# Attention, MLP and routed experts on one core: the products with v in one piece, behind the last copy, and routing logits as one accumulation

## Chip, cores and metric

The kernel runs on one core of one Trainium2 chip. The metric is device time in microseconds (us) of one execution, as a median of several runs. One execution was also recorded by the hardware profiler; every duration below comes from that one.

## What is computed

Three layers follow each other. Cut to what matters here:

```
# 1. attention, 4 batches x 8 heads, 576 tokens, head size 64, only the 32 largest scores of a row
scores = (q @ k.T) / 8
kth    = 32nd largest of each row
attn   = softmax(where(scores >= kth, scores, -1e9))
x      = attn @ v                                # then heads side by side: [2304, 512]

# 2. MLP
h = x @ w_in;  y = (h * clip(h + 3, 0, 6) / 6) @ w_out      # 512 -> 2048 -> 512

# 3. one expert of 8 for each token
logits = normalize(y) @ normalize(expert_emb).T / tau
e      = argmax(logits);  gate = softmax(logits)[e]
out    = gate * (relu(y @ w1[e]) @ w2[e])        # 512 -> 1024 -> 512
```

## The kernel before

**Units.** Attention is cut into 72 units: 64 take 128 query rows of a pair of heads, 8 take the 64 rows that are left over (rows 512 to 575) of two pairs of heads. A main loop (`while i < NU + 3 or moe or side`) starts one unit in each turn and keeps three in flight, one for each of the three score tiles `s` (`sbuf[i % 3]`).

**The path of one unit.** `scores` (L310) multiplies q with k on TensorE, in two halves `g` of 288 keys, into the PSUM tile `ps_sc`, of which there is one; ScalarE copies each half to `s` (L311). VectorE folds the halves (L317 to L321, reading `ps_sc`) and finds the 32 largest (`select`, L335, L341). `mask` pushes the others down (ScalarE L360, GpSimd L361) and takes the exponential (ScalarE L364). `transposes` scales the rows by the reciprocal of their sum (GpSimd L376), turns the nine blocks of 128 keys (two heads of 576 keys make 1152) on TensorE into `bank_t`, three at a time (L381), and ScalarE copies each three to `pt` (L382). `values` multiplies `pt` with v (L394) into a half of the PSUM bank `bank_a`; `finish` copies the sum to `x` (L412).

**The products with v.** A unit of 128 rows has ten, five for each head. Head `n` writes PSUM partitions 64n to 64n+63, so its weights are 64 columns wide, and the two heads use two halves of the array. Of the nine blocks of `pt`, head 0 reads 0 to 4 and head 1 reads 5 to 8 and 4. Blocks 0 to 2 come with the first copy, 3 to 5 with the second, 6 to 8 with the third. The loop begins with `k = 0`: block 0 (first copy), then block 5 (second copy), then 1, then 6 (third copy). A left-over unit has twenty products, on 64 moving columns each.

**The filler.** When 128 rows of x are complete, `push_group` puts nine steps of the MLP on a queue: `s1` (L433, into the two banks `bank_h`) and `s2` (L452, into `y`). Two steps go with each unit. After the last step come the routing steps r1 to r5 of that group, on a queue of their own. r1 transposes y to `yt` (L477, L479). r2 (L486) multiplies the normalized embeddings with `yt` in four products, each of 32 weight columns into its own 32 PSUM partitions; ScalarE copies the 128 rows to `lt` (L488). r3 (L492) adds the four parts by a product with the constant `fold`, which also brings tokens to the partitions, and VectorE copies the logits to `l_all` (L493). r4 and r5 find each token's place in its expert's list. There are 18 groups.

**What sets the order.** A list scheduler plays the program at build time and puts the instructions of each engine in a fixed order, which the engine follows in that order. What is ready goes by priority; `tc.high_priority(offset=...)` raises it. The offsets stand at the top: `FINISH = 500`, `MASK = 100`, `TURN = 300`, `VALUES = 300`, `SCORES = 500`, `SELECT = 600`, and `AHEAD = 600` for the steps between `s1` and `s2`.

**After attention.** The experts follow, the largest first: gathers of token rows (L631, L635), `stage1` (L734), `stage2` (L747), scattered rows of the output (L754).

Of the kernel before, what the change touches and what calls it, by code (L numbers as in the profile page):

```python
# [9 lines left out]
F32 = mybir.dt.float32  # L10
# [5 lines left out]
ALU = mybir.AluOpType  # L16
# [6 lines left out]
E, F2 = 8, 1024  # L23
# [20 lines left out]
PREP2 = 400  # L44
MASK = 100
TURN = 300
VALUES = 300
FINISH = 500
SCORES = 500
SELECT = 600  # L50
# [20 lines left out]
def layers(ctx: ExitStack, tc: tile.TileContext, qt, kt, v, w_in, w_out, embt, tau, w1, w2, out, y_dram, g_dram, x_dram, tbl, flag):  # L71
    nc = tc.nc
    exact = flag is None

    const = ctx.enter_context(tc.tile_pool(name="const", bufs=1))
    ident = const.tile([128, 128], F32, name="ident")
# [3 lines left out]
    ones = const.tile([128, 128], BF16, name="ones")  # L80
    tri = const.tile([128, 128], BF16, name="tri")
    ids = const.tile([128, NG, 2], I32, name="ids")
    ent = const.tile([128, 4, 32], F32, name="ent")
    fold = const.tile([128, E], F32, name="fold")
    acc = const.tile([128, E], BF16, name="acc")
    l_all = const.tile([128, NG, E], F32, name="l_all")
    ss_all = const.tile([128, NG], F32, name="ss_all")
# [3 lines left out]
    m1 = ctx.enter_context(tc.tile_pool(name="m1", bufs=1))  # L91
# [14 lines left out]
    bank_h = [ps_h.tile([128, 512], F32, name=f"bank_h{i}") for i in range(2)]  # L106
# [4 lines left out]
    def half_a():  # L111
        turn[0] ^= 1
        return bank_a[:, turn[0], :]
# [11 lines left out]
    def embed():  # L125
        onesf = xp.tile([128, 128], F32, tag="x", name="onesf")
        nc.vector.memset(onesf, 1.0)

        et = fs.tile([128, 4, E], F32, tag="df", name="et")
        nc.sync.dma_start(out=et, in_=embt.rearrange("(k p) e -> p k e", p=128))  # L130
        tb = fs.tile([128, 1], F32, tag="gt", name="tb")
        nc.sync.dma_start(out=tb, in_=tau.rearrange("(o t) -> o t", o=1).broadcast_to([128, 1]))
        sq = fs.tile([128, 4, E], F32, tag="gts", name="sq")
        nc.vector.tensor_tensor(sq, et, et, op=ALU.mult)
        pe = half_a()
        for k in range(4):
            nc.tensor.matmul(pe[:, :E], onesf, sq[:, k, :], start=(k == 0), stop=(k == 3))
        nr = fs.tile([128, E], F32, tag="nrm", name="nr")
        nc.scalar.activation(nr, pe[:, :E], AF.Sqrt)
        nc.vector.tensor_scalar(nr, nr, 1e-6, tb[:, 0:1], op0=ALU.add, op1=ALU.mult)  # L140
        nc.vector.reciprocal(nr, nr)
        nc.vector.memset(ent, 0.0)
        nc.vector.tensor_tensor(ent[:, :, 0:E], et, nr.unsqueeze(1).broadcast_to([128, 4, E]), op=ALU.mult)

    def setup():
        make_identity(nc, ident)
        nc.vector.tensor_tensor(fold, ident[:, 0:E], ident[:, 32:32 + E], op=ALU.add)
        for k in (2, 3):
            nc.vector.tensor_tensor(fold, fold, ident[:, 32 * k:32 * k + E], op=ALU.add)
        nc.vector.memset(half, 0.5)  # L150
        nc.vector.memset(ones, 1.0)
        nc.vector.memset(acc, 0.0)
        nc.gpsimd.iota(iota8, pattern=[[1, 8]], base=0, channel_multiplier=0, allow_small_or_imprecise_dtypes=True)
        nc.gpsimd.iota(ebase, pattern=[[STRIDE, 8]], base=0, channel_multiplier=0, allow_small_or_imprecise_dtypes=True)
        nc.gpsimd.affine_select(tri, ones, pattern=[[1, 128]], compare_op=ALU.is_gt, fill=0.0, base=0, channel_multiplier=-1)
        nc.gpsimd.iota(ids[:, :, 0], pattern=[[128, NG]], base=0, channel_multiplier=1)
        nc.gpsimd.iota(ids[:, 0:16, 1].rearrange("p (b t) -> p b t", b=4), pattern=[[S, 4], [128, 4]], base=0, channel_multiplier=1)
        for hf in range(2):
            nc.gpsimd.iota(ids[64 * hf:64 * hf + 64, 16:18, 1], pattern=[[2 * S, 2]], base=hf * S + 512, channel_multiplier=1)
        padt = xp.tile([128, E * STRIDE * 2 // 128], I32, tag="x", name="padt")  # L160
        nc.gpsimd.memset(padt, PAD)
        nc.sync.dma_start(out=tbl.rearrange("(p a) b -> p (a b)", p=128), in_=padt)
        zr = xp.tile([128, DM], F32, tag="x", name="zr")
        nc.vector.memset(zr, 0.0)
        nc.sync.dma_start(out=y_dram[NT:NT + 1, :], in_=zr[0:1, :])
        for g in (14, 15):
            nc.sync.dma_start(out=y_dram[128 * g:128 * g + 128, :], in_=zr)
        nc.sync.dma_start(out=g_dram[NT:NT + 128, :].rearrange("p o -> o p"), in_=zr[0:1, 0:128])
        embed()
# [196 lines left out]
    def transposes(i):  # L366


        e = sbuf[i % 3].rearrange("p n s -> p (n s)")
        pts[i] = ptp.tile([128, 9, 128], F32, tag="pt", name="pt")  # L370
        rv = sums.pop(i)
        nc.gpsimd.tensor_scalar(rv, rv, 1e-9, None, op0=ALU.add)
        nc.vector.reciprocal(rv, rv)  # L373
        for n in range(2):
            x = tile_of(i, n)
            nc.gpsimd.tensor_scalar(x, x, rv[:, n:n + 1], 1.0, op0=ALU.mult, op1=ALU.mult)  # L376
        for c in range(0, 9, 3):
            turn[1] ^= 1
            pp = bank_t[turn[1]]
            for k in range(3):  # L380
                nc.tensor.transpose(pp[:, 128 * k:128 * k + 128], e[:, 128 * (c + k):128 * (c + k) + 128], ident)  # L381
            nc.scalar.copy(pts[i][:, c:c + 3, :].rearrange("p k n -> p (k n)"), pp[:, :384])  # L382

    def values(i):


        u = units[i]
        pt = pts.pop(i)
        av = half_a()[:, :128]
        vs = [(V[u[1], u[3]], 0, 128)] if u[0] == "t" else [(V[u[1], u[2] + a], 64 * a, 64 * a + 64) for a in range(2)]  # L390
        for vt, c0, c1 in vs:
            for k in range(5):
                for n in range(2):
                    nc.tensor.matmul(av[64 * n:64 * n + 64, c0:c1], vt[:, k, 64 * n:64 * n + 64],  # L394
                                     pt[:, k + 5 * n if k < 4 else 4, c0:c1], start=(k == 0), stop=(k == 4))

        def finish():
            if u[0] == "r":
                _, b, p0 = u
                xq = mp.tile([128, 2, 64], F32, tag="xq", name="xq", bufs=1)  # L400
                nc.scalar.copy(xq.rearrange("d a t -> d (a t)"), av)
                nc.sync.dma_start(out=x_dram[p0:p0 + 2, :, 64 * b:64 * b + 64].rearrange("n d t -> d n t"), in_=xq)
                if b == B - 1 and p0 == 2:
                    for g in range(2):
                        X = xp.tile([128, 4, 128], F32, tag="x", name="x")
                        nc.sync.dma_start(out=X, in_=x_dram[:, :, 128 * g:128 * g + 128].rearrange("k d t -> d k t"))
                        push_group(X, 16 + g)
                return
            _, b, t, p = u
            if p == 0:  # L410
                xt[b, t] = xp.tile([128, 4, 128], F32, tag="x", name="x")
            nc.scalar.copy(xt[b, t][:, p, :], av)  # L412
            if p == 3:
                push_group(xt.pop((b, t)), 4 * b + t)
        return finish
# [8 lines left out]
    def push_group(X, g):  # L424

        state = {}
# [53 lines left out]
            state["yt"] = yt  # L480

        def r2():

            pl = bank_h[1][:, 256:384]
            for k in range(4):
                nc.tensor.matmul(pl[32 * k:32 * k + 32, :], ent[:, k, :], state["yt"][:, k, :], start=True, stop=True)  # L486
            state["lt"] = m1.tile([128, 128], F32, tag="yt", name="lt")
            nc.scalar.copy(state["lt"], pl)  # L488

        def r3():  # L490
            p2 = bank_h[0][:, 384:392]
            nc.tensor.matmul(p2, state["lt"], fold, start=True, stop=True)  # L492
            nc.vector.tensor_copy(l_all[:, g, :], p2)  # L493
            ix = sm.tile([128, 8], U32, tag="ix", name="ix")
            ixf = sm.tile([128, 1], F32, tag="ixf", name="ixf")
            oh = sm.tile([128, E], BF16, tag="oh", name="oh")
            mx = sm.tile([128, 8], F32, tag="mx", name="mx")
            nc.vector.max(mx, l_all[:, g, :])
            nc.vector.max_index(ix, mx, l_all[:, g, :])
            nc.vector.tensor_copy(ixf, ix[:, 0:1])  # L500
            nc.vector.tensor_scalar(oh, iota8, ixf, None, op0=ALU.is_equal)
            state["oh"] = oh
# [153 lines left out]
    if True:  # L656
# [5 lines left out]
        with tc.high_priority(offset=0):  # L662
            setup()
# [4 lines left out]
        while i < NU + 3 or moe or side:  # L668
# [9 lines left out]
            if 0 <= i - 2 < NU:  # L678
                with tc.high_priority(offset=MASK):
                    mask(i - 2)  # L680
                with tc.high_priority(offset=TURN):
                    transposes(i - 2)
                with tc.high_priority(offset=VALUES):
                    fin = [f for f in [values(i - 2)] if f]
# [220 lines left out]
```

## Time and profile before

| | |
|---|---|
| median of 3 runs | 1204.87 us (1203.87 to 1205.3) |
| the profiled execution | 1204.7 us, of which its span is 1202.8 us |
| busy in the span | PE 1080.5 us (90%), weight loads 918.6 (76%), DVE 808.6 (67%), ACT 737.1 (61%), POOL 696.9 (58%) |
| mean granted TensorE clock | 0.971 of 2.4 GHz |
| products with v (L394) | 1600 matmul records, 50.1 to 841.8 us |
| routing products (L486, L492) | 144 and 36 matmul records |

PE is TensorE's matmuls, PEld its weight loads, DVE is VectorE, ACT is ScalarE, POOL is GpSimd, SP is SyncE. A product of two float32 operands (L433, L394, L486, L492) shows as two matmul records, one of float32r operands (L310, L452) or a transpose (L381) as one. A record's duration runs past the start of the next record, since matmuls are pipelined; what one costs in a row of its kind is the distance from start to start.

### The profile page before, as it was taken

What the parts mean: (1) busy time and instruction counts of PE and PEld (TensorE: products, weight loads), DVE (VectorE), ACT (ScalarE), POOL (GpSimd) and SP (SyncE); (2) the same over time, 40 slices, a digit from 0 to 9 for tenths busy, and PEclk for the clock granted to TensorE, in tenths of its full rate; (3) what the DMA queues carried; (4) which work ended last, traced back from release to release, by engine and by line L of the source; (5) the groups of instructions that cost most, each with busy time, mean ns of one, the idle gap of its engine ahead of it and who ended that gap; (6) DMA issues with size and microseconds to landing.
All of it is one profiled execution on the core that took longest, in us unless ns stands there. A gap on an engine that the chain in (4) does not pass through costs nothing. (4 is left out here: it accounts for less than half of the span.)

```text
span 1202.8 us, 22847 instructions
## 1 busy us (share of the span) xinstructions
PE 1080.5 (90%) x7836; PEld 918.6 (76%) x7836; DVE 808.6 (67%) x2690; ACT 737.1 (61%) x1646; POOL 696.9 (58%) x982
## 2 busy tenths in 40 slices
PE   2347799999999999999999999999999799999993
PEld 2235578778888788888887888888888688888882
DVE  7999987788778858877788877874133344444440
ACT  5655676876767777776787776766344244444440
POOL 7977985967666786666797756754231442212200
PEclk9967999999999999999999999999999899999996
DMA  8443310230000221101022001000040564344530
GB/s 270 141 136 114 124 33 6 71 91 23 28 10 26 58 74 45 32 6 30 28 69 59 15 23 34 21 10 10 10 167 10 182 197 146 127 168 152 175 139 21
DMA packets 71783, 92.75 MB, mean 77 GB/s; under 512 B 18319, under 2 KB 44066, under 8 KB 71647
## 3 DMA queue, kind: packets, MB, share of 16 engines
q1 hardware_dynamic: 67007, 81.00, 21.4%
q0 software_dynamic: 4640, 10.10, 2.5%
q8 instruction: 66, 1.08, 0.4%
q14 instruction: 70, 0.57, 0.2%
HBM read 80.37 MB, written 11.32 MB: 76 GB/s over the span
## 5 line engine op out<-in xcount | busy, mean ns | idle before, releaser
L433 PE MATMUL bank_h<-x,win 128*128 128x128 f32 x2304 | 311.6, 279 | 16.5 <-ACT x L412 7.4
L433 PEld LDWEIGHTS bank_h<-x,win 128*128 128x128 f32 x2304 | 291.0, 193 | 38.4 <-ACT x L412 9.2
L361 POOL TENSOR_TENSOR s<-s,z 128x576 f32<-128x576 f32 x144 | 184.2, 1295 | 42.3 <-ACT z L360 40.0
L335 DVE MAX8 A<-left 128x8 f32<-128x288 f32 (+1 forms) x288 | 162.2, 596 | 0.0
L442 POOL TENSOR_TENSOR gl<-u,gh 128x256 fp32r<-128x256 f32 x144 | 106.7, 745 | 82.2 <-ACT gh L441 79.9
L394 PE MATMUL bank_a<-pt,vt 128*64 128x128 f32 (+1 forms) x1600 | 142.0, 279 | 13.5 <-ACT pt L382 13.4
L394 PEld LDWEIGHTS bank_a<-pt,vt 128*64 128x64 f32 x1600 | 93.5, 139 | 53.5 <-ACT pt L382 17.7
L310 PE MATMUL ps_sc<-kst,qh 128*128 128x288 f32 x256 | 86.5, 351 | 47.2 <-DVE left L321 13.2
L452 PE MATMUL y<-wh,gh 128*128 128x512 f32 x288 | 123.1, 427 | 0.8 <-ACT gh L441 0.8
L382 ACT COPY pt<-bank_t 128x384 f32<-128x384 f32 x216 | 100.4, 480 | 35.9 <-PE bank_t L381 34.9
L452 PE MATMUL y<-wh,gl 128*128 128x512 f32 x288 | 121.1, 421 | 0.1
L360 ACT ACTIVATE z<-s,zb 128x576 bf16<-128x576 f32 x144 | 107.4, 775 | 21.5 <-DVE zb L350 18.7
L381 PE MATMUL bank_t<-ident,s 128*128 128x128 f32 x648 | 110.8, 289 | 7.8 <-POOL s L376 7.7
L364 ACT ACTIVATE s<-s,nb 128x576 f32<-128x576 f32 x144 | 112.5, 782 | 8.1 <-POOL s L361 7.9
L311 ACT COPY s<-ps_sc 128x576 f32<-128x576 f32 x144 | 91.7, 637 | 38.9 <-PE ps_sc L310 32.3
L376 POOL TENSOR_SCALAR s<-s,sums 128x576 f32<-128x576 f32 x144 | 108.9, 767 | 10.9 <-DVE sums L373 9.7
L452 PE MATMUL y<-wl,gh 128*128 128x512 f32 x288 | 114.2, 396 | 0.0
L616 DVE TENSOR_TENSOR l<-a,h 128x1024 fp32r<-128x1024 f32 x64 | 76.9, 1223 | 52.7 <-ACT h L615 52.3
L317 DVE TENSOR_TENSOR ps_sc<-ps_sc,s 128x288 f32<-128x288 f32 x72 | 33.3, 462 | 105.0 <-ACT s L311 104.9
L438 ACT ACTIVATE u<-bank_h,half 128x256 f32<-128x256 f32 x144 | 67.9, 475 | 58.1 <-PE bank_h L433 55.7
L439 DVE SCALAR_TENSOR_TENSOR u<-u,bank_h 128x256 f32<-128x256 f32 x144 | 59.3, 413 | 60.6 <-ACT u L438 59.8
L381 PEld LDWEIGHTS bank_t<-ident,s 128*128 128x128 f32 x648 | 75.3, 144 | 29.6 <-issue 14.9
(227 smaller groups left out, 2457.1 us busy)
## 6 DMA issues: line engine op xcount, KB each, us to landing
a<-in_moe_w_dram SPq DMA_DIRECT2D x64, 512.0 KB, 8.5
kraw<-in_k_dram SPq DMA_DIRECT2D x64, 144.0 KB, 2.4
qraw<-in_q_dram SPq DMA_DIRECT2D x64, 128.0 KB, 2.2
w<-in_moe_w_in_dram SPq DMA_DIRECT2D x32, 256.0 KB, 3.2
w<-in_moe_w_out_dram SPq DMA_DIRECT2D x32, 256.0 KB, 2.9
vt<-in_v_dram SPq DMA_DIRECT2D x16, 320.0 KB, 2.9
y_dram<-ysb SPq DMA_DIRECT2D x18, 256.0 KB, 2.1
qraw<-in_q_dram SPq DMA_DIRECT2D x16, 64.0 KB, 2.3
```

Of the source, the lines that this page charges most:

```text
L311: nc.scalar.copy(s[:, :, HS * g:HS * g + HS], ps[:, :, :HS])
L335: nc.vector.max(A[:, n, 8 * r:8 * r + 8], src[:, n, :w])
L360: nc.scalar.activation(zb_[n], s, AF.Relu, bias=zb[:, n:n + 1], scale=-BIG)
L361: nc.gpsimd.tensor_tensor(s, s, zb_[n], op=ALU.subtract)
L364: nc.scalar.activation(s, s, AF.Exp, bias=nb[:, n:n + 1], scale=SCALE, accum_out=so[:, n:n + 1])
L376: nc.gpsimd.tensor_scalar(x, x, rv[:, n:n + 1], 1.0, op0=ALU.mult, op1=ALU.mult)
L381: nc.tensor.transpose(pp[:, 128 * k:128 * k + 128], e[:, 128 * (c + k):128 * (c + k) + 128], ident)
L382: nc.scalar.copy(pts[i][:, c:c + 3, :].rearrange("p k n -> p (k n)"), pp[:, :384])
L394: nc.tensor.matmul(av[64 * n:64 * n + 64, c0:c1], vt[:, k, 64 * n:64 * n + 64], pt[:, k + 5 * n if k < 4 else 4, c0:c1], start=(k == 0), s ...
L433: nc.tensor.matmul(ph[:, a, :], win[:, k, 128 * f:128 * f + 128], X[:, k, :], start=(k == 0), stop=(k == 3))
L442: nc.gpsimd.tensor_tensor(gl, u, gh.bitcast(F32), op=ALU.subtract)
L452: nc.tensor.matmul(state["y"], x[:, a, :], w[:, f, :], start=(f == 0 and n == 0), stop=(f == 15 and n == 2))
```

## The change

`VALUES` goes from 300 to 1200, above every other offset. The loop over the five blocks of a head takes them as 3, 2, 1, 0, 4 with head 1 first, so that the first product reads block 8, which comes with the third copy.

r2 now has `yt` as weights, 128 columns wide, and the embeddings `ent` as the moving operand, 8 columns, in one accumulation of four products into `p2`, which lies in `bank_h[1]` where `pl` lay. ScalarE's copy `lt`, the product with `fold` and the making of `fold` are gone, and r3 begins with VectorE's copy to `l_all`. Lines behind the change move up by 4 to 8: L394 becomes L390, L310 L305, L381 L376, L433 L429, L452 L448, L486 L481.

```diff
-VALUES = 300
+VALUES = 1200
...
-    ent = const.tile([128, 4, 32], F32, name="ent")
-    fold = const.tile([128, E], F32, name="fold")
+    ent = const.tile([128, 4, E], F32, name="ent")
...
-        nc.vector.memset(ent, 0.0)
-        nc.vector.tensor_tensor(ent[:, :, 0:E], et, nr.unsqueeze(1).broadcast_to([128, 4, E]), op=ALU.mult)
+        nc.vector.tensor_tensor(ent, et, nr.unsqueeze(1).broadcast_to([128, 4, E]), op=ALU.mult)
...
-        nc.vector.tensor_tensor(fold, ident[:, 0:E], ident[:, 32:32 + E], op=ALU.add)
-        for k in (2, 3):
-            nc.vector.tensor_tensor(fold, fold, ident[:, 32 * k:32 * k + E], op=ALU.add)
...
-            for k in range(5):
-                for n in range(2):
+
+            for o, k in enumerate((3, 2, 1, 0, 4)):
+                for n in (1, 0):
                     nc.tensor.matmul(av[64 * n:64 * n + 64, c0:c1], vt[:, k, 64 * n:64 * n + 64],
-                                     pt[:, k + 5 * n if k < 4 else 4, c0:c1], start=(k == 0), stop=(k == 4))
+                                     pt[:, k + 5 * n if k < 4 else 4, c0:c1], start=(o == 0), stop=(o == 4))
...
         def r2():
-
-            pl = bank_h[1][:, 256:384]
+            p2 = bank_h[1][:, 256:264]
             for k in range(4):
-                nc.tensor.matmul(pl[32 * k:32 * k + 32, :], ent[:, k, :], state["yt"][:, k, :], start=True, stop=True)
-            state["lt"] = m1.tile([128, 128], F32, tag="yt", name="lt")
-            nc.scalar.copy(state["lt"], pl)
+                nc.tensor.matmul(p2, state["yt"][:, k, :], ent[:, k, :], start=(k == 0), stop=(k == 3))
+            state["p2"] = p2
 
         def r3():
-            p2 = bank_h[0][:, 384:392]
-            nc.tensor.matmul(p2, state["lt"], fold, start=True, stop=True)
-            nc.vector.tensor_copy(l_all[:, g, :], p2)
+            nc.vector.tensor_copy(l_all[:, g, :], state["p2"])
```

How this moves instructions stands in the built order of TensorE. In the order of before the 800 products with v stand in 205 pieces, with other products between them: 61 of one product, 51 of two, 46 of seven, and 47 of other sizes. In the order of the change they stand in 72 pieces, one for each unit.

TensorE, the products with v of the 40th unit. The names `s_...` are the score tile that is transposed, `bank_t_...` the two banks that take it. Before:

```order
L433 MATMUL bank_h_118<-x,win 128x128
L394 MATMUL bank_a<-pt,vt 64x128
L381 MATMUL bank_t_121<-ident,s_144 128x128 x3
L394 MATMUL bank_a<-pt,vt 64x128 x2
L310 MATMUL ps_sc<-kst,qh 128x288
...
L433 MATMUL bank_h_119<-x,win 128x128 x3
L394 MATMUL bank_a<-pt,vt 64x128 x7
L452 MATMUL y<-wh,gh 128x512
```

The same unit with the change:

```order
L376 MATMUL bank_t_120<-ident,s_143 128x128 x3
L429 MATMUL bank_h_118<-x,win 128x128 x3
L305 MATMUL ps_sc<-kst,qh 128x288
...
L390 MATMUL bank_a<-pt,vt 64x128 x10
L448 MATMUL y<-wh,gh 128x512
```

One product, two and seven became ten in a row, behind the last transposes, three MLP products and four of scores.

TensorE, the 31st unit, whose products with v, with the change, follow its last three transposes with nothing between them; a routing step r2 stands behind them. Before:

```order
L394 MATMUL bank_a<-pt,vt 64x128
L381 MATMUL bank_t_122<-ident,s_144 128x128 x3
L452 MATMUL y<-wh,gh 128x512
L452 MATMUL y<-wl,gh 128x512
L394 MATMUL bank_a<-pt,vt 64x128 x2
L452 MATMUL y<-wh,gl 128x512
```

With the change:

```order
L473 MATMUL bank_h_117<-ident,ysb 128x128 x4
L376 MATMUL bank_t_121<-ident,s_143 128x128 x3
L390 MATMUL bank_a<-pt,vt 64x128 x10
L481 MATMUL bank_h_118<-ent,yt 128x8 x4
L429 MATMUL bank_h_117<-x,win 128x128 x3
```

The ten products moved next to the transposes whose copy they read. Counted over the order of the change, four units stand so (the 18th, 22nd, 31st and 54th); from the seventh unit on, six more have four instructions in between, ten have five to eight, and the other 46 have more.

TensorE, a routing step r2 and r3 in the middle of attention. Before:

```order
L381 MATMUL bank_t_122<-ident,s_144 128x128 x2
L486 MATMUL bank_h_119<-yt,ent 32x128 x4
L433 MATMUL bank_h_118<-x,win 128x128 x3
...
L492 MATMUL bank_h_118<-fold,lt 128x8
L433 MATMUL bank_h_119<-x,win 128x128 x3
```

With the change:

```order
L305 MATMUL ps_sc<-kst,ql 128x288
L481 MATMUL bank_h_118<-ent,yt 128x8 x4
L429 MATMUL bank_h_117<-x,win 128x128 x8
```

The second product is gone, and the four products of r2 are 128 weight columns wide and 8 long.

## Rows read from the trace of the kernel before

**Rows 1.** Busy time by stretch: the stretch in us, its length, busy us (and records) of PE, PEld, DVE, ACT and POOL, the granted clock, the DMA share, GB/s.

```profile
0.00:150.00 150.00, 76.74 (x425) 59.15 (x426) 141.59 (x402) 88.32 (x213) 127.09 (x179) 0.86 0.50 157
500.00:700.00 200.00, 197.34 (x1572) 167.59 (x1572) 157.38 (x612) 148.58 (x349) 139.60 (x207) 1.00 0.13 36
900.00:1203.00 303.00, 270.01 (x1591) 235.62 (x1590) 121.35 (x203) 119.05 (x193) 71.13 (x74) 0.95 0.38 131
```

**Rows 2.** What TensorE waited for from 150 to 890 us: who waited, for whom, us in total, times, longest.

```profile
PE bank_h L433 <- ACT lt L488: 2.4, 2, 1.3
PE bank_a L394 <- ACT pt L382: 2.1, 4, 0.7
PE bank_t L381 <- POOL s L376: 1.2, 1, 1.2
```

**Rows 3.** What VectorE waited for from 200 to 800 us.

```profile
DVE ps_sc L317 <- ACT s L311: 96.0, 44, 5.1
```

**Rows 4.** The timeline of TensorE's matmuls: start and length in us, line, operation, out and in, weights and moving operand, number of records in a row. The 40th unit's products with v, in three pieces.

```profile
500.51 0.38 PE L433 MATMUL bank_h<-x,win 128*128 128x128 f32 x2
500.82 0.43 PE L394 MATMUL bank_a<-pt,vt 128*64 128x128 f32 x2
501.18 0.55 PE L381 MATMUL bank_t<-ident,s 128*128 128x128 f32 x3
501.66 0.44 PE L394 MATMUL bank_a<-pt,vt 128*64 128x128 f32 x4
502.03 0.40 PE L310 MATMUL ps_sc<-kst,qh 128*128 128x288 f32 x1
...
502.66 0.83 PE L433 MATMUL bank_h<-x,win 128*128 128x128 f32 x6
503.42 1.09 PE L394 MATMUL bank_a<-pt,vt 128*64 128x128 f32 x14
504.43 0.50 PE L452 MATMUL y<-wh,gh 128*128 128x512 f32 x1
504.77 0.40 PE L452 MATMUL y<-wl,gh 128*128 128x512 f32 x1
```

**Rows 5.** The same view where a unit's ten products, 20 records, stand in one piece.

```profile
720.48 0.40 PE L452 MATMUL y<-wl,gh 128*128 128x512 f32 x1
720.71 0.40 PE L452 MATMUL y<-wh,gl 128*128 128x512 f32 x1
721.04 1.31 PE L394 MATMUL bank_a<-pt,vt 128*64 128x128 f32 x20
722.28 0.94 PE L433 MATMUL bank_h<-x,win 128*128 128x128 f32 x6
722.98 1.31 PE L310 MATMUL ps_sc<-kst,zq 128*128 128x288 f32 x8
```

**Rows 6.** The same view, two stretches of full-width products alone.

```profile
327.95 0.61 PE L433 MATMUL bank_h<-x,win 128*128 128x128 f32 x4
328.40 0.82 PE L381 MATMUL bank_t<-ident,s 128*128 128x128 f32 x6
329.05 0.39 PE L433 MATMUL bank_h<-x,win 128*128 128x128 f32 x2
...
505.01 0.30 PE L310 MATMUL ps_sc<-kst,qh 128*128 128x288 f32 x1
505.14 0.29 PE L310 MATMUL ps_sc<-kst,ql 128*128 128x288 f32 x1
```

**Rows 7.** PE and PEld of the products with v (L394) from 0 to 150 us: busy us and records of each, granted clock, DMA share, GB/s.

```profile
0.00:150.00 150.00, 16.65 (x126) 10.42 (x126) 0.86 0.50 157
```

**Rows 8.** The timeline of TensorE's matmuls around one r2 (L486).

```profile
601.04 0.29 PE L310 MATMUL ps_sc<-kst,ql 128*128 128x288 f32 x1
601.26 0.43 PE L486 MATMUL bank_h<-yt,ent 128*32 128x128 f32 x8
601.62 2.05 PE L433 MATMUL bank_h<-x,win 128*128 128x128 f32 x16
603.50 0.82 PE L381 MATMUL bank_t<-ident,s 128*128 128x128 f32 x6
```

**Rows 9.** The same around one product of r3 (L492).

```profile
799.12 0.61 PE L433 MATMUL bank_h<-x,win 128*128 128x128 f32 x4
799.56 0.29 PE L492 MATMUL bank_h<-fold,lt 128*128 128x8 f32 x2
799.70 0.47 PE L433 MATMUL bank_h<-x,win 128*128 128x128 f32 x2
800.01 0.60 PE L381 MATMUL bank_t<-ident,s 128*128 128x128 f32 x4
```

**Rows 10.** The timeline of TensorE and ScalarE: the third copy of the 40th unit (its transposes start at 501.18), and the third transposes and copy of the unit behind it.

```profile
501.77 0.48 ACT L382 COPY pt<-bank_t 128x384 f32<-128x384 f32 x1 [1.40 <-PE bank_t L381]
509.81 0.55 PE L381 MATMUL bank_t<-ident,s 128*128 128x128 f32 x3
511.60 0.47 ACT L382 COPY pt<-bank_t 128x384 f32<-128x384 f32 x1
```

**Rows 11.** What TensorE waited for from 0 to 150 us.

```profile
PE bank_a L394 <- ACT pt L382: 11.3, 5, 3.1
PE bank_t L381 <- POOL s L376: 6.5, 3, 3.9
```

## Prediction

> **What bounds the kernel now.** I first read busy time by stretch. From 500 to 700 us TensorE is busy 197.34 of 200 us at a granted clock of 1.00, while VectorE is busy 157.38, ScalarE 148.58 and GpSimd 139.60; from 0 to 150 us it is the other way round, VectorE 141.59 and TensorE 76.74 [rows 1]. So the start belongs to VectorE and its suppliers, and from about 150 us to the end of the MLP near 890 us TensorE's own queue sets the pace. The experts, from 900 us, hold nothing that the change touches; they move forward or back as a whole. The list of waits confirms the middle: TensorE waited there for the copies of `pt` 2.1 us in all, for `lt` 2.4, for GpSimd's scaling 1.2 [rows 2]. VectorE in turn waited 96.0 us between 200 and 800 us for ScalarE's copy of the scores, which waits for TensorE [rows 3]. An instruction that TensorE can do without is therefore worth its whole time in the middle, until something else is late.
>
> Busy time does not show what is dear on TensorE, since it is near 100% in any case. I therefore read its timeline from start to start.
>
> **Prices of full-width products.** Four records of L433 take 328.40 - 327.95 = 0.45 us, 0.1125 each; six transposes 329.05 - 328.40 = 0.65, 0.108 each; one record of scores 505.14 - 505.01 = 0.13 [rows 6]; one of L452 720.71 - 720.48 = 0.23 [rows 5].
>
> **The products with v: what a piece costs.** The 40th unit's 20 records stand in pieces of 2, 4 and 14. From 500.51 to 504.77 us TensorE also did 8 records of L433 (0.90), 3 transposes (0.325), 4 of scores (0.52) and one of L452 (0.23). The rest, 4.26 - 1.975 = 2.285 us, is the products with v [rows 4]. Where 20 records stand in one piece, 720.71 to 722.98 us holds one L452 (0.23) and 6 of L433 (0.675) beside them; the rest is 2.27 - 0.905 = 1.365 us [rows 5]. Same work, 0.92 us less, for two pieces less: 0.46 us for each entry to and exit from the half-width products, together with the product that then runs without its partner in the other half. Entry and exit can be seen alone: from the last L452 to the first L394 are 0.33 us where 0.23 are usual [rows 5], and between the two L452 behind the piece of 14 lie 0.34 [rows 4].
>
> The order of the change has 72 pieces instead of 205, so 133 x 0.46 = 61 us of TensorE's time go. 126 of the 1600 records lie before 150 us [rows 7], where TensorE was idle half the time; that 8% is worth nothing. **56 us** remain on the path.
>
> **The products with v: the new wait.** All ten now stand behind the third copy. In the 40th unit the third transposes start at 501.18 [rows 4] and their copy ends at 501.77 + 0.48 = 502.25 us, 1.07 us later; the next unit's start at 509.81 and their copy ends at 511.60 + 0.47 = 512.07, 2.26 us later, since ScalarE was busy [rows 10]. The three transposes themselves are 0.33 of that, so a unit with nothing in between lets TensorE wait 0.74 to 1.93 us, and with it the scores and MLP products queued behind, on which ScalarE's copies and VectorE's selection depend. By the order of the change four units have nothing between (3.0 to 7.7 us), six have four instructions of at least 0.43 us together (6 x 0.2 to 6 x 1.5, or 1.2 to 9), ten have five to eight, near 0.9 us (0 to 10), the other 46 more. Ends: 4 and 27 us. I take **6**, near the low end, since TensorE waited for this copy only 2.1 us in four waits in this stretch [rows 2]. Of this wait little existed before, when two products or three could start with the earlier copies, so I count it in full.
>
> **What is late next.** If TensorE needs 8% less time, VectorE's 157.38 of 200 us become 157.38 of about 184, 85%; its wait for scores, 96.0 us in 600, is what pays [rows 1, 3]. It is no bound yet, but leads shrink, and some units' scaled scores will come after TensorE is ready for the transposes. Such a wait is 6.5 / 3 = 2.2 us where it happened at the start [rows 11], and happened once in the middle, for 1.2 us [rows 2]. One unit in twelve of the 66 behind the start gives 5.5 x 2.2 = **12 us**. The ends are 0 (TensorE keeps its order's slack) and one unit in four, 36 us. I choose low, because one wait moves all of TensorE's later work and so restores the lead of the units in flight.
>
> **The routing logits.** r2's eight narrow records cost, from 601.04 to 603.50 us, 2.46 less one of scores (0.13) and 16 of L433 (1.80): 0.53 us [rows 8]. r3's product: 799.12 to 800.01 us holds 6 records of L433, 0.675 of 0.89, so 0.215 us for its two records, 0.11 each [rows 9]. That record is 128 weight columns wide and 8 long, as the eight new ones of r2 are; they cost 8 x 0.11 = 0.86 us. Per group 0.86 - 0.53 - 0.215 = +0.12 us, in 18 groups **+2 us**. The wait for `lt`, 2.4 us, goes [rows 2]; VectorE's copy now holds the bank `bank_h[1]` in its place until it has read, so I count the waits as **0**, between -2.4 and +3. ScalarE is spared 18 copies and VectorE a few instructions at the start, both beside TensorE's work.
>
> A rule speaks against this edit. The rows show that four 32-column products save no time once entry and exit are counted. The Trainium skill, page "TensorEngine Tiling (Array Packing)", section "Theoretical Speedup", gives up to 4x for a dimension of at most 32; by it the packed r2 would be a quarter of 0.86 us, and the edit would cost (0.86 - 0.215 - 0.215) x 18 = 8 us instead of 2, an estimate. The rows of this case decide, and nothing below uses that figure.
>
> **Sum.** -56 + 6 + 12 + 2 + 0 = -36 us. The profiled execution took 1204.7 us, its span and 1.9 us around it, and the median of the runs is 1204.87, so no correction between them is needed: **1169 us**.
>
> **The rivals.**
>
> Full gain. TensorE's slack covers the new waits: -56 + 2 + 3 for the four units with nothing in between gives 1154 us; about 1146 to 1158 us if the 2.4 us for `lt` and a part of the middle's other waits go too. For it: the middle has hardly any waits now. Against it: leads that were measured under a slower TensorE. 17%.
>
> Another chain takes over half the way. VectorE, ScalarE and GpSimd together need as long for a unit as before, and TensorE waits for the scaled scores or for `ps_sc` to be read. With one unit in five, 13 x 2.2 = 29 us instead of 12: 1186 us; 11 to 19 such units give 1181 to 1199. For it: VectorE at 79% now. Against: it waits itself. 14%.
>
> Slower. The head of TensorE's queue stands behind the third copy in nearly every unit, because ScalarE, in its own fixed order, does not come to it. It decides from (56 - 12 - 2) / 66 = 0.64 us of wait per unit. In the early stretch five such waits took 11.3 us, 2.3 each [rows 11]; at 1 us in each of 66 units the sum is -56 + 12 + 2 + 66 = +24, or 1229 us. Against it: 46 units have nine instructions or more in between. 5%.
>
> No effect. The distances on the timeline hold time that TensorE would lose anyway, or the experts' own inputs (weights, gathers) come no earlier and the experts end when they did: within 2.4 us of 1205. Against: the first loads of the experts hang on the end of attention in the program. 4%.
>
> **How the numbers follow.** The forecast, 1159 to 1181 us, has 60%, full gain 17%, half 14%, slower 5%, no effect 4%. The range of 1148 to 1190 us takes in most of the two neighbours. A difference of under 0.2% (2.4 us) cannot be told from none by measurement. Faster by more: 60 + 17 + 14 = 91%; within: 4%; slower: 5%.
>
> **What would show it.** In the changed profile: every unit's L390 is one group of 20 or 40 records; TensorE's records from 150 us to the last s2 product (L448) span some 35 us less; its waits for `pt` L377 grow to some 8 us, those for GpSimd's scaling and for `ps_sc` by some 12; VectorE's wait for scores falls. r2's eight records (L481) lie about 0.11 us apart. I am wrong if a piece's cost stays in the timeline with the pieces gone (entry and exit were not the cause), or if the waits of TensorE in the middle exceed 40 us.

## The result and the profile after

The changed kernel takes 1210.62 us, median of 20 runs, against 1203.29 us of the kernel before in 20 runs: a ratio of 1.0056, interval 1.0042 to 1.0071, slower by 0.56%. The profiled execution took 1209.1 us with a span of 1207.4 us, 4.6 us more than before's 1202.8. The forecast was 1169 us.

I read busy time by stretch first, as in [rows 1]. The changed kernel:

```profile
0.00:150.00 150.00, 76.88 (x441) 62.23 (x441) 140.69 (x393) 88.46 (x213) 125.21 (x178) 0.82 0.50 155
150.00:300.00 150.00, 135.34 (x1055) 120.81 (x1056) 112.13 (x426) 105.01 (x248) 108.82 (x158) 0.92 0.17 47
300.00:500.00 200.00, 189.64 (x1578) 169.22 (x1578) 158.51 (x617) 149.23 (x350) 144.22 (x214) 0.98 0.15 39
500.00:700.00 200.00, 187.53 (x1569) 168.19 (x1564) 153.17 (x597) 149.75 (x349) 140.81 (x208) 0.99 0.13 36
700.00:890.00 190.00, 186.34 (x1525) 168.84 (x1525) 119.18 (x453) 120.66 (x276) 105.90 (x153) 1.00 0.09 29
150.00:890.00 740.00, 698.84 (x5716) 627.06 (x5717) 542.99 (x2090) 524.65 (x1220) 499.75 (x731) 0.98 0.13 37
```

The kernel before, the middle as a whole:

```profile
150.00:890.00 740.00, 725.15 (x5757) 616.30 (x5755) 542.65 (x2082) 524.98 (x1231) 495.95 (x728) 1.00 0.13 37
```

In these 740 us TensorE did nearly the same work as before: 5716 records against 5757, and r3's 32 are among those that are gone. Its busy time fell by 725.15 - 698.84 = 26.3 us, and its idle time rose by as much, so the middle is hardly shorter. The column behind POOL's is the second finding: the granted clock, 1.00 throughout the middle before, is 0.92, 0.98, 0.99 and 1.00. As the clock has two levels, 0.92 over 150 us means 0.08 x 2 x 150 = 24 us at half speed (1.2 GHz); with 8 and 4 us of the next two stretches it is near 36 us (34.1 without the rounding).

What TensorE waited for from 150 to 890 us, as in [rows 2]; the longest single wait is the last number:

```profile
PE bank_a L390 <- ACT pt L377: 10.4, 8, 2.7
PE ps_sc L305 <- DVE left L316: 8.6, 6, 4.0
PE y L448 <- ACT gh L437: 3.8, 5, 1.3
PE ps_sc L305 <- ACT s L306: 3.5, 3, 1.6
PE bank_h L429 <- DVE zb L345: 3.4, 1, 3.4
PE bank_h L429 <- DVE u L435: 3.0, 3, 2.2
```

All rows of this list sum to 42.1 us, before to 14.2. The new wait for `pt` is a quarter of it; the others are waits for what VectorE and ScalarE deliver.

The timeline of TensorE's matmuls shows the part of the change that worked, a unit's ten products in one piece, then a wait and what came behind it, and an r2 at full clock:

```profile
506.00 0.29 PE L305 MATMUL ps_sc<-kst,ql 128*128 128x288 f32 x1
506.22 1.31 PE L390 MATMUL bank_a<-pt,vt 128*64 128x128 f32 x20
507.46 0.50 PE L448 MATMUL y<-wh,gh 128*128 128x512 f32 x1
507.80 0.39 PE L448 MATMUL y<-wl,gh 128*128 128x512 f32 x1
...
210.03 0.49 PE L376 MATMUL bank_t<-ident,s 128*128 128x128 f32 x3
210.35 0.64 PE L473 MATMUL bank_h<-ident,ysb 128*128 128x128 f32 x4
213.50 1.56 PE L390 MATMUL bank_a<-pt,vt 128*64 128x128 f32 x20 [2.50 <-ACT pt L377]
214.99 0.61 PE L305 MATMUL ps_sc<-kst,qh 128*128 128x288 f32 x1
215.39 0.44 PE L305 MATMUL ps_sc<-kst,ql 128*128 128x288 f32 x1
215.63 0.44 PE L305 MATMUL ps_sc<-kst,qh 128*128 128x288 f32 x1
...
216.11 1.71 PE L481 MATMUL bank_h<-ent,yt 128*128 128x8 f32 x8
217.68 3.73 PE L429 MATMUL bank_h<-x,win 128*128 128x128 f32 x16
221.09 0.45 PE L305 MATMUL ps_sc<-kst,qh 128*128 128x288 f32 x1
...
518.17 0.96 PE L481 MATMUL bank_h<-ent,yt 128*128 128x8 f32 x8
518.98 1.81 PE L429 MATMUL bank_h<-x,win 128*128 128x128 f32 x14
```

From 506.00 to 507.80 us lie the unit's ten products, one record of scores (0.13) and one of L448 (0.23): 1.80 - 0.36 = 1.44 us, entry and exit included, where three pieces took 2.285 [rows 4]. The pieces' cost did go with the pieces. The unit at 213 us waits 2.50 us. From then on score products lie 0.24 us apart instead of 0.13, eight records of r2 take 1.57 us instead of 0.81, and sixteen of L429 take 3.41 us instead of 1.80 [rows 6]. The two last differences alone are 2.4 us, as much as the wait.

ScalarE's timeline at this place shows why the third copy of `pt` was late:

```profile
210.18 0.77 ACT L249 CAST kst<-kraw 128x288 fp32r<-128x288 f32 x2
210.84 0.41 ACT L285 CAST qh<-qraw 128x256 fp32r<-128x256 f32 x1
211.15 0.64 ACT L306 COPY s<-ps_sc 128x576 f32<-128x576 f32 x1
211.68 0.77 ACT L249 CAST kst<-kraw 128x288 fp32r<-128x288 f32 x2
212.35 0.64 ACT L470 ACTIVATE yt<-ysb 128x512 f32<-128x512 f32 x1
...
212.97 0.47 ACT L377 COPY pt<-bank_t 128x384 f32<-128x384 f32 x1
```

The transposes were through near 210.5 us, and the copy stood behind this work in ScalarE's fixed order. TensorE's queue had only four transposes to put in between.

The experts did not move as a whole. Their first product starts at 894.0 us and their last at 1186.0:

```profile
L726 PE MATMUL ph<-xh__10262,h x64: 262/280/557, 894.0 to 964.6; 128*128 128x256 f32 x32, 128*128 128x224 f32 x32
L739 PE MATMUL po<-l,hh x176: 387/395/402, 923.0 to 1186.0; 128*128 128x512 f32 x136, 128*96 128x512 f32 x16, 128*80 128x512 f32 x8, 128*48 128x512 f32 x8
```

Before, the same products started at 896.9 and 1181.4 us:

```profile
L734 PE MATMUL ph<-xh__10315,h x64: 261/280/553, 896.9 to 971.5; 128*128 128x256 f32 x32, 128*128 128x224 f32 x32
L747 PE MATMUL po<-l,hh x176: 387/395/482, 926.2 to 1181.4; 128*128 128x512 f32 x136, 128*96 128x512 f32 x16, 128*80 128x512 f32 x8, 128*48 128x512 f32 x8
```

So the first part ends 2.9 us earlier and the experts take 7.5 us longer (292.4 us to the last product's end against 284.9). TensorE's waits of the changed kernel from 900 to 1207 us lead to the gathers:

```profile
PE pxt L627 <- DMA xg<-y_dram,idt: 13.6, 5, 4.2
```

Before, this row read 8.8 us in five waits. Behind two of the gathers the clock fell again: the stretches 1000 to 1050 and 1050 to 1100 us have 0.97 each, where the kernel before had 1.00.

### The profile page after: what moved, and what is told of

It reads as the page before. It is cut to its first block, busy times and chain, and to the rows that moved or that the text cites. A ratio compares the mean times of both kernels' runs of the same rounds, so it can differ in the third digit from the quotient of the medians.

```text
span 1207.4 us, 22745 instructions
## 1 busy us (share of the span) xinstructions
PE 1056.1 (87%) x7800; PEld 935.3 (77%) x7800; DVE 806.1 (67%) x2686; ACT 733.4 (61%) x1628; POOL 699.7 (58%) x982
## 5 line engine op out<-in xcount | busy, mean ns | idle before, releaser
L429 PE MATMUL bank_h<-x,win 128*128 128x128 f32 x2304 | 312.9, 284 | 17.1 <-DVE u L435 8.1
L429 PEld LDWEIGHTS bank_h<-x,win 128*128 128x128 f32 x2304 | 296.7, 198 | 32.2 <-DVE u L435 12.0
L305 PE MATMUL ps_sc<-kst,qh 128*128 128x288 f32 x256 | 89.2, 360 | 58.1 <-DVE left L316 34.7
L448 PE MATMUL y<-wh,gh 128*128 128x512 f32 x288 | 123.2, 428 | 3.8 <-ACT gh L437 3.8
L376 PE MATMUL bank_t<-ident,s 128*128 128x128 f32 x648 | 108.4, 285 | 17.0 <-ACT pt L377 10.8
L448 PE MATMUL y<-wh,gl 128*128 128x512 f32 x288 | 119.1, 414 | 0.7 <-POOL gl L438 0.5
L448 PE MATMUL y<-wl,gh 128*128 128x512 f32 x288 | 114.3, 397 | 0.0
L390 PE MATMUL bank_a<-pt,vt 128*64 128x128 f32 (+1 forms) x1600 | 101.6, 278 | 11.7 <-ACT pt L377 11.6
L305 PEld LDWEIGHTS ps_sc<-kst,qh 128*128 128x128 f32 x256 | 53.3, 208 | 71.6 <-issue 22.2
L390 PEld LDWEIGHTS bank_a<-pt,vt 128*64 128x64 f32 x1600 | 84.2, 143 | 27.2 <-ACT pt L377 15.5
L376 PEld LDWEIGHTS bank_t<-ident,s 128*128 128x128 f32 x648 | 80.6, 146 | 28.9 <-ACT pt L377 13.0
```

The lines of the kernel that those rows point to most:

```text
L305: nc.tensor.matmul(ps[:, n, :HS], t, kk[:, HS * g:HS * g + HS], start=(o == 0), stop=(o == len(parts) - 1))
L429: nc.tensor.matmul(ph[:, a, :], win[:, k, 128 * f:128 * f + 128], X[:, k, :], start=(k == 0), stop=(k == 3))
L448: nc.tensor.matmul(state["y"], x[:, a, :], w[:, f, :], start=(f == 0 and n == 0), stop=(f == 15 and n == 2))
```

## The experiments

My theory after the result had three parts: the block order removes the pieces and is worth some 40 us of TensorE's time; the waits that replace them cost their length and a stretch at half clock on top; the edits of priority and routing add waits and bring nothing. The rivals: TensorE's time is no longer what counts, because another chain sets the pace; r2's result holds the bank `bank_h[1]` until VectorE reads it; and chance of one execution.

**One part at a time.** The priority alone:

```diff
-VALUES = 300
+VALUES = 1200
```

> Before with only the priority of the products with v raised from 300 to 1200; 194 pieces in TensorE's built order instead of 205. Theory 'waits and clock' (TensorE's saved time is real, and new waits plus half-clock time after them gave it back): 11 pieces less are worth 5 us, so 1198 to 1206 us. Theory 'pace' (attention goes at the pace of a loop through the other engines, about 10.4 us a unit, whatever TensorE saves): within 0.3% of before, 1200 to 1207. The two do not differ here; the run tells what the priority does alone.

The block order alone:

```diff
-            for k in range(5):
-                for n in range(2):
+            for o, k in enumerate((3, 2, 1, 0, 4)):
+                for n in (1, 0):
...
-                    start=(k == 0), stop=(k == 4))
+                    start=(o == 0), stop=(o == 4))
```

> Before with only the order of the five blocks changed (3, 2, 1, 0, 4, head 1 first), priority 300, old routing; 87 pieces instead of 205, and by the built order only 5 units from the seventh on have less than 1.2 us of TensorE work between their third transposes and their first product with v, against 15 in the change. 'Waits and clock': most of 118 x 0.46 = 54 us is kept since few units meet the wait, 1155 to 1185 us, with under 25 us of waits from 150 to 890 us and hardly any half clock there. 'Pace': 1198 to 1208 us, with TensorE's idle time grown by 25 us or more.

The routing alone, r2 and r3 as in the diff of the change:

> Before with only the routing edit; 214 pieces in the built order. Theory 'routing' (the routing edit is what costs the change its gain, by holding a bank of the MLP or by its eight wide weight loads): 1225 us or more. 'Waits and clock' and 'pace' both: +2 us for r2, +4 for nine pieces more, 1203 to 1213 us.

Block order and priority with the old routing:

> The change without the routing edit: block order and priority 1200, old routing; 72 pieces; 7 units from the seventh on have less than 1.2 us between third transposes and first product. 'Waits and clock': 1155 to 1190 us. 'Pace': 1198 to 1210 us. 'Routing': at least 25 us below the change, as in the first case, and then e3_routing has to be slow; if e3 is not slow and this run is fast, it is the built order of the change, not the routing step's own cost.

The whole change with `VALUES = 300`:

> The change with the priority put back to 300, so block order and routing edit together; 86 pieces, and 12 units from the seventh on have less than 1.2 us of TensorE work between third transposes and first product with v (5 without the routing edit). Theory 'routing' (the routing edit costs some 20 us by its own work, whatever stands around it): e2_blocks plus 20, 1208 to 1216 us. Theory 'waits and clock' (a wait of TensorE of some 1.3 us or more costs itself and then a stretch at half clock; which edits bring such waits is a matter of the built order): between e2 and the change, 1193 to 1210 us, and the excess over e2 shows as waits and half clock, not as time of r2.

Measured, each with the kernel before on the same chip (pieces: groups of products with v in the order, before 205):

```
kernel              us        before    ratio [interval]          pieces
priority            1213.74   1204.71   1.0083 [1.0067, 1.0098]   194
block order         1191.77   1204.71   0.9882 [0.9868, 0.9897]    87
routing             1226.49   1204.71   1.0180 [1.0167, 1.0194]   214
order + priority    1201.44   1204.71   0.9967 [0.9954, 0.9980]    72
order + routing     1209.17   1203.64   1.0047 [1.0030, 1.0064]    86
```

The block order is the part that gains, 1.2%. The priority takes 10 us back although it leaves fewer pieces. The routing edit, forecast at 2 us, costs 22 us alone; on top of order and priority it costs 9 us by the medians and 11 by the ratios, which take out the difference between the chips, and on top of the order 17 and 20.

The forecasts of these runs came out badly. 'Waits and clock', my own theory, had put the first four lower than they came; only order + routing lies in its range, and in that of 'routing' as well. The routing alone came where 'routing' put it, order + priority where 'pace' put it, and the first two lie in no range. Nor were the block order's waits under 25 us: to the first expert product the trace has 33.9 us of them, and 23.9 us at half clock.

In the trace of the routing edit alone, TensorE's timeline shows the pattern again, where nothing of the products with v was changed:

```profile
223.86 1.06 PE L428 MATMUL bank_h<-x,win 128*128 128x128 f32 x8
228.24 3.29 PE L428 MATMUL bank_h<-x,win 128*128 128x128 f32 x16 [3.33 <-DVE u L434]
231.46 0.48 PE L389 MATMUL bank_a<-pt,vt 128*64 128x64 f32 x2
```

Sixteen records take 3.2 us instead of 1.8. The granted clock of this run from 150 to 880 us is 0.98, while its waits are no longer in sum than before's (15.9 against 16.3 us to the first expert product); the single waits are longer, up to 3.33 us.

**Order alone.** `SIDE`, the priority of the routing steps, goes from 100 to 300 in the kernel before; the instructions stay the same and only their order changes. Then the routing edit on this order:

> Before with SIDE (the priority of the routing steps) 300 instead of 100: the same instructions, 217 pieces, another order. 'Routing': nothing of the routing's work changes, so within 0.3% of before plus 5 us for twelve pieces more, 1203 to 1212 us. 'Waits and clock': the order alone can bring waits above 1.3 us where before has none from 150 to 890 us; then 1208 to 1228 us, with the granted clock below 1.00 in some 200 us stretch.

> The routing edit alone (as e3_routing) in another built order: SIDE 300 instead of 100, 212 pieces. It is compared with e6_side300, 1210.3 us, the same priority with the old routing. Theory 'routing' (the edit's own work costs some 20 us): 1225 to 1235 us again. Theory 'waits and clock' (the edit's own cost is 2 us and the 22 us of e3 came with that order): it may land elsewhere, 1200 to 1222 us, and what it has above e6 shows as waits and half clock.

Another order of the same instructions gave 1210.25 against 1203.64 us, 1.0058 [1.0041, 1.0075], as large as the whole result, with 217 pieces and no half clock:

```profile
150.00:880.00 730.00, 713.09 (x5636) 602.79 (x5635) 538.01 (x2062) 517.54 (x1216) 490.29 (x721) 1.00 0.12 33
```

Twelve pieces more, at the 0.38 us that is worked out below, are 4.6 of these 6.6 us. The time lies in both ranges, but the half clock that 'waits and clock' expected is not there, so the run fits 'routing' better. With the routing edit it is 1222.63 against 1205.02 us, 1.0155 [1.0130, 1.0181], just outside both ranges. So the routing edit costs 12 us here too, 7.9 of them among the experts (292.3 us against 284.4).

**Is it chance?** The changed kernel once more:

> The change once more, for a second profile. 'Waits and clock': 35 to 48 us of waits and 25 to 45 us at half clock from 150 to 890 us, with the long waits at the same places (products with v near 213, 276, 318 and 411 us, scores near 241, 598), and the expert stage 5 us or more longer than before's 285 us, with gather waits of 3 us or more near 1016 and 1088 us. If those were chance, they stand elsewhere.

1210.6 us, and the waits of the new execution from 150 to 890 us are the same ones:

```profile
PE bank_a L390 <- ACT pt L377: 10.5, 8, 2.7
PE ps_sc L305 <- DVE left L316: 8.4, 6, 3.8
```

They stand at the same places (near 213, 241, 276, 318, 411 and 598 us among them), so they belong to the order that was built and not to one execution.

**Does TensorE's time still count?** The product of `gl` with `wh` is left out of the MLP's second layer, 288 records of 0.23 us, 66 us, once with the block order and once in the kernel before; the logits and the output are then less exact.

```diff
-                for n, (x, w) in enumerate(((gh, wh), (gh, wl), (gl, wh))):
+                for n, (x, w) in enumerate(((gh, wh), (gh, wl))):
```

> e2_blocks with the third of the MLP's second products left out (gl with wh, 288 records of 0.23 us, 66 us of TensorE): part of the computation is missing. Theory 'pace' (a loop through the other engines gives each unit about 10.4 us whatever TensorE saves): 1175 to 1195 us, TensorE's waits grown by 50 us or more. 'Waits and clock': 1130 to 1160 us, two thirds or more of the 66 us gained.

> Before with the same products left out. 'Pace' with a loop just below TensorE's present time: 1185 to 1205 us. 'Waits and clock': 1140 to 1165 us. The distance to e7_blocks_less_mlp tells whether the pieces are still worth their 0.46 us when TensorE has less other work: 30 us or more if TensorE alone sets the time, under 10 us if the gain is used up by waits.

With the block order 1141.39 us (0.9484 [0.9468, 0.9500]): 50 of the 66 us are gained (48 by the ratios). Before with the same edit 1170.86 us (0.9733 [0.9703, 0.9763]): 33 of 66, between the ranges of the two theories. Had another chain set the pace behind the block order, the first number would have been near nothing. The rival falls as the main cause. The pieces keep their worth as well: the two kernels are 29.5 us apart. But TensorE's time comes through only by half to three quarters. In the kernel before, the edit adds 12.8 us of waits and 5.5 us of loss at half clock to the first expert product, beside 13 pieces more; with the block order it adds 4.5 and 4.9 us, and its clock is 0.97:

```profile
150.00:880.00 730.00, 688.53 (x5816) 612.87 (x5814) 566.19 (x2162) 539.43 (x1274) 506.00 (x745) 0.97 0.15 42
```

**Is it r2's bank?** Order and routing with `p2` in the other bank; the same with r2's products moved into r3, so that nothing is held between the two; and that on the routing edit alone.

```diff
-            p2 = bank_h[1][:, 256:264]
+            p2 = bank_h[0][:, 384:392]
```

> e5_blocks_routing with the sum of the routing products in bank_h[0] instead of bank_h[1]; 91 pieces. Theory 'bank' (the sum waits in an MLP bank from r2 to r3): still a bank of the MLP with a step between, so about as e5, 1204 to 1214 us. Theory 'order' (only the built order differs): anywhere between e2 and 10 us above e5, 1190 to 1220.

> e5_blocks_routing with products and copy in one step, sum in bank_h[0]; 101 pieces, 15 more than e5, worth 6 us. 'Bank': most of the 17 us above e2 goes, 1192 to 1202 us. 'Order': no reason for it to go, 1198 to 1220 us, and the excess stands in waits, half clock and the expert stage, not at the routing's own instructions.

> e3_routing with products and copy in one step, sum in bank_h[0]; 218 pieces. 'Bank': most of the 22 us above before goes, 1204 to 1213 us. 'Order': 1208 to 1230 us.

Measured 1205.70 against 1205.61 us, 1.0005 [0.9995, 1.0016]; 1214.30, 1.0055 [1.0038, 1.0071]; and 1231.91, 1.0213 [1.0191, 1.0235]. The other bank gives back about 0.4%, but where nothing is held between r2 and r3 the edit costs as much as ever, although the 'bank' theory had put these two runs at 1192 to 1202 and 1204 to 1213 us. So holding the bank is not the main cause. The three builds also differ in their order (91, 101 and 218 pieces).

**Better versions.** The block order with `VALUES = 200`, and with `MASK = 500` instead of 100:

> e2_blocks with the priority of the products with v lowered to 200: 111 pieces instead of 87, and 10 instead of 14 units from the seventh on with under 2 us between third transposes and first product. 'Waits and clock': 24 pieces more cost 24 x 0.38 = 9 us; waits and half clock fall by some 10 us at most: 1183 to 1200 us. If pieces did not matter it would be at or below e2, 1180 to 1191.

> e2_blocks with the priority of the mask steps raised from 100 to 500: 90 pieces, the same instructions. 'Waits and clock': GpSimd's scaling and the transposes come earlier relative to TensorE's other work, waits from 150 to 890 us stay at or below e2's 35 us, 1183 to 1198 us. If block order helps only by a lucky order, this one can be at 1200 to 1210.

1201.38 us (0.9974 [0.9955, 0.9992]) and 1190.86 us (0.9880 [0.9855, 0.9905]). The first, just above its forecast, is 10 us slower than the block order alone, near the 9 us that its 24 pieces more were priced at. The second equals the block order alone within the interval; these two beat the kernel before by 1.2% and the changed one by 1.7%.

## Why the prediction was wrong, step by step

The step that failed leads from saved instructions to saved time. The sum priced a new wait at its length alone and had no term for the half clock behind it; that is 15 us. It also priced the pieces 11 us too high, took the experts as unmoved, which is 7.5 us, and the waits 6 us too low. Together these are nearly all of the 41 us between the forecast of -36 us and the +4.6 us of the profiled spans.

I split the time from 150 us to the first expert product of the profiled executions into waits of TensorE, loss at half clock, products with v and r2, and the other products at their full-clock distances. The loss is an estimate: the distances of the records in half-clock stretches, less the mean distance at full clock of the same products in the same run. It cannot exceed half of the time at half clock, which is 34.1 us in the changed kernel. The column of v and r2 is what remains; it holds the cost of entry and exit. The 40.6 us of waits leave out one that began before 150 us, which the 42.1 above count. The last column is the experts, from their first product to the last one's end.

```
                     to expert   waits   half clock   v and r2   others   experts
before                 746.9      16.3       0         157.9     572.7    284.9
changed                744.0      40.6      15.1       119.1     569.2    292.4
order + priority       734.0      37.7      10.3       112.3     573.7    293.3
block order            733.2      33.9       9.7       115.6     574.0    287.7
routing                762.8      15.9      10.8       167.4     568.7    288.6
```

**The pieces, forecast -56: -45 us.** Order and priority without the routing edit shows it: 112.3 - 157.9 = -45.6 us for 119 pieces fewer behind 150 us, 0.38 each. The block order alone gives 42.3 us for 104 pieces, 0.41 each. The mechanism was right and the 0.46 us of one pair of units too high; and 14 of the 133 pieces lay before 150 us, more than the 8% of the records.

**Routing, forecast +2: +2 in its own products.** v and r2 together grew by 6.8 us from order + priority to the whole change, the others lost 4.5 with r3's product. r2's eight records take 0.81 us at full clock (518.17 to 518.98), near the 0.86 that I priced. Yet the edit as a whole costs 9 to 22 us in four pairs. In the routing edit alone 10.8 us of that stand in half clock, 3.7 us in the experts, and near 4 us in ten pieces more behind 150 us. On top of order and priority the waits grew by 2.9 us, as "0, between -2.4 and +3" allowed, and the half clock by 4.8 us. On top of the block order 7.6 us stand in waits and 7.3 us in the experts. So "waits 0" failed in the last pair; in the other two it was the half clock without a term.

**The priority,** which the sum gave no cost of its own, adds to the block order 3.8 us of waits, 0.6 at half clock and 5.6 among the experts, and its fewer pieces give back 3.3.

**The new wait, forecast +6: +8 us.** The wait for `pt` went from 2.1 [rows 2] to 10.4 us, as put, within the ends of 4 and 27.

**"What is late next", forecast +12: 16 us, and 15 us more that had no term.** All waits grew by 40.6 - 16.3 = 24.3 us, 16 beside the one for `pt`, within the ends of 0 and 36. That the size fits is in part luck, since the price came from waits for GpSimd's scaling, and these grew only from 1.2 to 1.8 us. Waits for `ps_sc`, which the prediction named but did not price, grew from 3.8 to 12.9 us, and the rest came at the MLP's banks. And a wait was priced at its length. Eight stretches at half clock, six of them behind or within a wait of 1.3 us or more, cost another 15.1 us. This is the largest miss, and "an instruction that TensorE can do without is worth its whole time" fails with it: the gaps that its removal opens cost more than they are long. The loss is read from rows; no run isolates it with all else equal.

**"They move forward or back as a whole", forecast 0: +7.5 us.** TensorE's idle time among the experts grew by 4.2 us, at the gathers, and its busy time by 3.3 us at half clock. The order of the experts' gathers is built with all the rest, and it did change: in GpSimd's trace the gathers of `xg` stand at other places among the scatters of the output than before. In the block order alone they stand as before, and its experts take 287.7 us.

The sum: -45.6 for the pieces, +1.0 in the other products, +2.3 for routing, +24.3 for waits and +15.1 for half clock are -2.9 us to the first expert product, as measured, and +7.5 stand behind it: +4.6 us of span.

Two readings in the prediction were off without moving its sum. That "four 32-column products save no time once entry and exit are counted" is not what its rows show: r2's eight narrow records took 0.53 us [rows 8] where eight full-width records of L433 take 0.90. And six units with 0.43 us in between start at a wait of 0.31 us, not 0.2.

Of the rivals, "slower" had the third copy at the head of nearly every queue; it was eight waits. "Another chain" had the right direction, but the product left out shows TensorE still sets most of the pace. My bound for being wrong, waits over 40 us in the middle, was passed with 42.1. VectorE's wait for scores did fall, from 96.0 to 85.5 us.

What stays open: why the priority and the routing edit, which touch so little, led to worse orders each time, in waits, half clock or gathers. Another order of the same instructions alone gave 0.6%, of which the pieces explain most; a general answer may not exist, and no run decides it.

## What to carry to other kernels

When an engine is near 100% busy and its order is fixed in advance, price what you remove at its time, and every wait that opens at its length plus the half-clock stretch behind it; here the second was some three fifths of the first. Test the parts of such a change apart: one part was worth 1.2%, and the two beside it took more than that back. And measure what a mere reordering does, here 0.6%, since one build of an edit below that size does not tell the edit from its order.

## What the runs showed of the hardware

TensorE's clock stayed at 1.00 in the middle of the kernel before, where its longest wait was 1.3 us. In the changed kernel there were eight stretches at half clock from 150 us to the first expert product. One followed the wait that ended at 213.50 us, of 2.50 us: the stretch 213.50 to 221.10 us has a granted clock of 0.56 although TensorE was busy in all of it.

```profile
210.00:213.50 3.50, 1.00 (x10) 0.70 (x8) 2.15 (x7) 3.50 (x11) 2.52 (x4) 1.00 0.35 117
213.50:221.10 7.60, 7.60 (x49) 7.27 (x49) 6.02 (x28) 4.20 (x9) 4.48 (x6) 0.56 0.28 75
221.30:231.30 10.00, 10.00 (x102) 9.55 (x103) 9.04 (x35) 8.48 (x21) 8.52 (x11) 1.00 0.29 74
```

So here the clock was full in the idle stretch itself, low in the busy one behind it, and full again after that: the idle time was paid afterwards. The Trainium skill, page "TensorE: Matmul & The Clock Gate", section "What's actually happening", calls the low clock the default state, from which activity releases the engine; the fall behind idle time and the return to 1.00 under full activity fit that.

The length of a wait does not decide it alone. Of eleven waits of 1.3 us or more, seven had such a stretch behind or around them (two share one) and four had none, one of 2.44 us among these. And two of the eight stretches followed shorter waits, at 269.0 and 460.2 us. There TensorE was at the eight records of r2, which are 8 columns long, or had just done them. At the first place:

```profile
266.22 0.66 PE L473 MATMUL bank_h<-ident,ysb 128*128 128x128 f32 x4 [0.56 <-ACT ysb L462]
268.24 1.18 PE L481 MATMUL bank_h<-ent,yt 128*128 128x8 f32 x8 [0.59 <-ACT yt L475]
269.28 1.63 PE L429 MATMUL bank_h<-x,win 128*128 128x128 f32 x6
```

From 269.03 to 272.44 us the granted clock is 0.50. The second execution of the changed kernel shows both places again. So the 1.3 us that my theory named are no limit. The new r2 may itself have a part in the half clock that came with the routing edit; no run isolates it.
